# ConvNeXt-V2 block on one core: three of eleven blocks' hidden layer stored whole and read back, the rest rebuilt whole

## The chip, the cores and the metric

The kernel runs on one core of one Trainium2 chip. The metric is the device time of a whole execution in microseconds (us). The kernel before takes 1508.77 us, the median of 3 executions (1508.57 to 1510.78).

A **ratio** below is the mean time of one kernel's fast runs over the mean of the other's fast runs of the same rounds. It is therefore not quite the ratio of the medians that are quoted beside it. Its 95 % interval stands in brackets. "Same" means within 2 %.

## The reference

The input is 512 x 512 pixels of 96 channels in bf16; the hidden layer has 384 features.

```python
def reference(x, dw, w1, w2, grn_gamma, grn_beta):
    ...                                          # out = 3x3 depthwise convolution of x
    h = _layernorm(out, axis=-1)
    h = jnp.einsum('bhwc,ce->bhwe', h, w1)
    h = _gelu(h)
    gx = jnp.sqrt((h * h).sum(axis=(1, 2), keepdims=True) + 1e-6)
    nx = gx / (gx.mean(axis=-1, keepdims=True) + 1e-6)
    h = grn_gamma * (h * nx) + grn_beta + h
    h = jnp.einsum('bhwe,ec->bhwc', h, w2)
    return x + h
```

The sum in `gx` runs over the whole picture. No output can be made before the hidden layer of every pixel has been seen once, and neither kernel holds that layer (128 blocks of 1.57 MB) on the chip. So the kernel has two phases, and the question is what of the hidden layer phase 2 reads back and what it rebuilds.

## The kernel before

The picture is cut into 128 blocks of four rows, which are 2048 pixels. A block's hidden layer consists of four pixel quarters (`t`, `m`) of three feature chunks (`j`), each chunk a tile of 128 features by 512 pixels.

**Phase 1** works a slot at a time. In a slot, PE convolves one block (the input comes transposed from DVE) and makes the first product of a block a few slots older, ACT evaluates the gelu, and the sums of squares are taken. For quarters that have features on the partitions ("channel-major", `cm_quads`), DVE takes them with `bn_stats`. For the others PE takes them with a product of the tile with itself (`gram`). The normalized convolution yn goes to DRAM and comes back channel-major. In this kernel every block keeps one quarter of the hidden layer in DRAM:

```python
def cm_quads(q):
    return 2 if is_res(q) else 3          # is_res: the two last blocks
def kept_quads(q):
    return 2 if is_res(q) else 1
...
# one slot of phase 1, in this order
conv(0); unit(0, 2); unit(2, 1)
squares(0)                                # 2 statistics entries on DVE
conv(1, False)
turn_x(s + 2)                             # DVE transposes the input of a later slot
unit(3, 1); unit(4, 2)
squares(1)                                # 2 entries
...
squares(2)                                # 2 entries
...
squares_rest()                            # entries of the third quarter: 3
store = put_out                           # one quarter to g_dram in the next slot
```

**Phase 2** takes the blocks in turn. It loads the kept quarter (`gl`), yn of the three other quarters and the input (`xr`), rebuilds three quarters on PE and ACT (`gr`), makes the second product (`O`) and adds input and bias. The sum of input and bias (`xb`) is POOL's work:

```python
def stage_load(n, sq, pq):
    ...
        kept = late.gl.tile([128, 1, NCH, QW], bf16, name="gl")
        (pq if q % 3 == 0 else sq).dma_start(
            out=kept[:].rearrange("p t j w -> p (t j w)"), in_=g_dram[q])
        ynt = yn_ring[v]
        sq.dma_start(out=ynt[:, :, kept_quads(q) * 128:], in_=yn_rows(q))
    xr = late.xr.tile([128, PXP, C], bf16, name="xr")      # 5 buffers
    pq.dma_start(out=xr[:], in_=x[0, r0:r0 + GR]...)

def stage_xb(q, pq, bias):
    xb = late.xb.tile([128, PXP, C], f32, name="xb")
    pq.tensor_tensor(out=xb[:], in0=grp[q]["xr"][:], in1=bias[...], op=ALU.add)
...
for n, q in enumerate(ORDER):             # phase 2
    if n + PRE < NBLK:
        stage_load(n + PRE, nc.sync, nc.gpsimd)
    if n + 2 < NBLK:
        stage_xb(ORDER[n + 2], nc.gpsimd, B2c)
    ...
    o_sb = stage_mm2(n, q)                # second product; pace() puts rebuilding between
```

Of the kernel before, what the change touches and what calls it, by code (L numbers as in the profile page):

```python
# [12 lines left out]
GR = 4  # L13
# [5 lines left out]
RES = 2  # L19

# [33 lines left out]
def kernel(  # L54
# [29 lines left out]
    g_dram = dram.tile([NBLK, 128, NCH * QW], bf16, name="g_dram")  # L84
# [5 lines left out]

    def cm_quads(q):
        return 2 if is_res(q) else 3

    def kept_quads(q):
        return 2 if is_res(q) else 1
# [16 lines left out]
    def yn_rows(q):  # L112
        k = kept_quads(q) * 128
        return yn_dram[q:q + 2].rearrange("q c (r w) -> (q c) r w", r=GR)[0:128, :, k:]
# [29 lines left out]
    grp = {}  # L144
    res_g = {q: prepool.tile([128, 2, NCH, QW], bf16, name=f"resg{q}") for q in range(NBLK - RES, NBLK)}
# [7 lines left out]
    ORDER = list(range(NBLK - RES, NBLK)) + list(range(NBLK - RES))  # L153

    class late:
        pass
# [3 lines left out]
    with ExitStack() as p1:  # L160
        pe, dve, act, pool, sp = (InOrder(tc, e) for e in (nc.tensor, nc.vector, nc.scalar, nc.gpsimd, nc.sync))
        gshpool = p1.enter_context(tc.tile_pool(name="gsh", bufs=3))
        gmpool = p1.enter_context(tc.tile_pool(name="gm", bufs=3))
# [70 lines left out]
        def stage_load(n, sq, pq):  # L234
            q = ORDER[n]
            v = (ORDER[0] + n) % NYT
            r0 = q * GR
            if is_res(q):
                kept, ynt = res_g[q], ynts[q]
            else:  # L240
                kept = late.gl.tile([128, 1, NCH, QW], bf16, name="gl")
                (pq if q % 3 == 0 else sq).dma_start(
                    out=kept[:].rearrange("p t j w -> p (t j w)"), in_=g_dram[q])
                ynt = yn_ring[v]
                sq.dma_start(out=ynt[:, :, kept_quads(q) * 128:], in_=yn_rows(q))
# [3 lines left out]
            grp[q] = dict(kept=kept, ynt=ynt, xr=xr)  # L249

        def recompute_units(q):
            nk = kept_quads(q)
            ynt = grp[q]["ynt"]

            def fresh(j):
                if j == 0:
                    grp[q]["made"] = late.gr.tile([128, NCH, (NQ - 1) * QW], bf16, name="gr")
                def half(U, t0, t1):
                    for t in range(t0, t1):
                        pe.matmul(quad_out(U[:, t - t0, :]), lhsT=w1p[:, j * 128:(j + 1) * 128],  # L260
                                  rhs=quad(ynt[:], t), start=True, stop=True)
                    act.activation(out=grp[q]["made"][:, j, (t0 - nk) * QW:(t1 - nk) * QW],
                                   in_=U[:, :t1 - t0, :].rearrange("p k w -> p (k w)"), func=ACTF.Gelu_apprx_tanh)

                if not is_res(q):
                    half(late.psU2.tile([128, NQ - 1, QW], f32, name="U2"), nk, NQ)
                elif j % 2:
                    half(banks(1), nk, nk + 1)
                    half(banks(1), nk + 1, NQ)
                else:  # L270
                    half(banks(2), nk, NQ)

            return [lambda j=j: fresh(j) for j in range(NCH)]
# [9 lines left out]
        def stage_mm2(n, q):  # L283
            kept, made, xb = grp[q]["kept"], grp[q]["made"], grp[q]["xb"]
            nk = kept_quads(q)
            GQ = QW // 128
            o_sb = late.o.tile([128, PXP, C], bf16, name="o_sb")
            for sub in range(NSUB):
                O = late.psO.tile([128, GPS, C], f32, name="O")
                for gl_ in range(GPS):  # L290
                    gg = sub * GPS + gl_
                    for j in range(NCH):
                        t, c = gg // GQ, gg % GQ * 128
                        if t < nk:
                            lhsT = kept[:, t, j, c:c + 128]
                        else:
                            c += (t - nk) * QW
                            lhsT = made[:, j, c:c + 128]
# [4 lines left out]
                if n == NBLK - 1:  # L303
                    out_part(q, o_sb, sub)
# [18 lines left out]
        def advance(target, upto):  # L323
            while made[0] < total and made[0] < target and todo[made[0]] < upto:
                n = todo[made[0]]
                if not waiting:
                    waiting.extend(recompute_units(ORDER[n]))
# [530 lines left out]
        if store:  # L858
            store()
# [102 lines left out]
```

## Time and profile before

| kernel before | value |
|---|---|
| time, median | 1508.77 us |
| span of the profiled execution | 1504.8 us |
| mean granted clock of PE | 0.993 |
| busy: PE, DVE, ACT, POOL | 94 %, 79 %, 96 %, 87 % |
| last transpose of an input starts | 863.6 us |
| copy of `B2c` starts, after which phase 2's adds can start | 969.8 us |
| last add of an output tile starts | 1501.2 us |

The page's line of the chain that ended last gives each engine's share of the span:

```profile
POOL 22%; PE 20%; ACT 12%; DVE 10%; DMA 8%; issue 3%; SPq 3%; POOLq 0%; ACTq 0%
```

Every compute engine is on that chain; none can be neglected. The stretches, groups and instructions that carry the argument are shown in the prediction. One wait of phase 2 (1060 to 1460 us; total, times, longest) shows who is late there:

```profile
DVE o_sb L32 <- POOL xb L279: 87.4, 81, 3.5
```

### The profile page before, as it was taken

Reading aid. Unit: us, or ns where it says so; the run is one execution under the profiler, and the core shown is the slowest. Engines: PE = TensorE matmul, PEld = TensorE weight load, DVE = VectorE, ACT = ScalarE, POOL = GpSimd, SP = SyncE. Lnnn points to the kernel's source line nnn. Section 1 sums busy time; section 2 is a strip of 40 time slices with the busy share of each in tenths; the row PEclk is TensorE's granted clock in tenths of the full one; section 3 lists DMA queues with packets and bytes.
Section 4 is the critical chain, followed back from the end, with each engine's and each line's share of the span. In section 5 each row is a group of like instructions: output and inputs, shape, how many; then the busy total and the mean of one; then the engine's idle time right before and its main releaser. Section 6 shows DMA issues by size and latency. Waiting matters only on the chain.

```text
span 1504.8 us, 54858 instructions
## 1 busy us (share of the span) xinstructions
PE 1415.3 (94%) x23110; PEld 815.8 (54%) x23110; DVE 1193.5 (79%) x2149; ACT 1450.9 (96%) x1699; POOL 1309.6 (87%) x934
## 2 busy tenths in 40 slices
PE   8888999999999999999999987799999999999998
PEld 3434444444444444444444443477777777676776
DVE  7759999999999999999999999755555555455555
ACT  7898999999999999999999999899999999899997
POOL 3469899999999999989999987199999999899998
PEclk9999999999999999999999999999999999999999
DMA  6568787888888888888888777799999999999996
GB/s 177 175 199 255 227 257 241 252 260 242 245 256 250 256 260 244 252 252 249 248 265 243 221 216 252 237 340 388 378 391 385 380 378 376 362 367 382 378 378 237
DMA packets 235181, 427.10 MB, mean 284 GB/s; under 512 B 34006, under 2 KB 148278, under 8 KB 234934
## 3 DMA queue, kind: packets, MB, share of 16 engines
q1 hardware_dynamic: 219972, 356.59, 73.7%
q0 software_dynamic: 13600, 66.86, 11.7%
q8 instruction: 181, 2.97, 0.8%
q14 instruction: 66, 0.54, 0.1%
q10 hardware_dynamic: 1362, 0.15, 0.1%
HBM read 272.78 MB, written 150.72 MB: 281 GB/s over the span
## 4 chain that ended last, share of the span: by engine, by line
POOL 22%; PE 20%; ACT 12%; DVE 10%; DMA 8%; issue 3%; SPq 3%; POOLq 0%; ACTq 0%
POOL xb L279 13%; PE U L32 10%; PE O L32 9%; DVE bst L32 7%; ACT gsh L32 6%; ACT gm L32 4%; SPq L32 3%; POOL yn L32 3%; DMA ynT<-yn_dram 2%; DMA yn_dram<-yn 2%; ACT y_bf L32 2%; POOL ysq L32 2%; DMA xin<-in_x_dram 2%; DVE xT L32 2%; POOL xr L247 1%
## 5 line engine op out<-in xcount | busy, mean ns | idle before, releaser
L32 PE MATMUL U<-ynT,w1p 128*128 128x512 bf16 x2292 | 651.7, 381 | 37.3 <-ACT gsh L32 9.6
L32 ACT ACTIVATE gr<-U 128x1536 bf16<-128x1536 f32 (+1 forms) x386 | 519.3, 1449 | 13.5 <-PE U L32 12.8
L32 DVE BATCH_NORM_STATS2 bst<-gsh 128x6 f32<-128x512 bf16 x756 | 465.4, 673 | 20.0 <-ACT gsh L32 19.5
L32 DVE TENSOR_TENSOR o_sb<-O,xb 128x384 bf16<-128x384 f32 x512 | 277.7, 556 | 254.1 <-PE O L32 157.5
L32 POOL TENSOR_TENSOR yn<-y_bf,rbc 128x1536 bf16<-128x1536 bf16 x126 | 391.5, 3109 | 70.7 <-DMA rbc<-r_dram 26.4
L279 POOL TENSOR_TENSOR xb<-xr,B2c 128x1536 f32<-128x1536 bf16 x126 | 394.8, 3135 | 34.0 <-DVE B2c L32 27.2
L32 ACT ACTIVATE gm<-U 128x512 bf16<-128x512 f32 (+1 forms) x640 | 419.8, 803 | 3.9 <-PE U L32 3.8
L32 ACT ACTIVATE gsh<-U 128x1024 bf16<-128x1024 f32 x504 | 375.0, 872 | 5.7 <-PE U L32 4.1
L32 PE MATMUL Y<-xT,Wq 64*32 64x511 bf16 (+1 forms) x8694 | 321.7, 387 | 21.4 <-ACT y_bf L32 9.5
L32 POOL TENSOR_TENSOR ysq<-y_bf 128x1536 bf16<-128x1536 bf16 x114 | 314.1, 2756 | 11.4 <-ACT y_bf L32 11.4
L32 PEld LDWEIGHTS <-w1p 128*128 128x128 bf16 x2292 | 183.1, 98 | 241.3 <-issue 141.5
L32 PEld LDWEIGHTS <-gr 128*128 128x128 bf16 x4584 | 236.8, 98 | 106.3 <-issue 21.2
L32 PE MATMUL O<-W2s,gr 128*128 128x96 bf16 x4584 | 257.2, 206 | 11.5 <-DVE o_sb L32 11.0
L32 DVE BATCH_NORM_STATS2 bst<-gm 128x6 f32<-128x512 bf16 x378 | 232.9, 671 | 0.2 <-ACT gm L32 0.2
L32 PEld LDWEIGHTS <-Wq 64*32 64x32 bf16 x9216 | 113.1, 90 | 199.1 <-issue 150.5
L32 ACT ACTIVATE y_bf<-Y 128x1536 bf16<-128x1536 f32 x121 | 188.0, 1554 | 8.5 <-DMA gam_bf<-in_grn_gamma_dram 4.4
L32 DVE STREAM_TRANSPOSE xT<-xin 128x576 f32<-128x576 f32 (+1 forms) x256 | 181.2, 748 | 0.0
L32 PEld LDWEIGHTS <-gm 128*128 128x128 bf16 x1560 | 99.3, 98 | 84.9 <-issue 52.2
L32 PE MATMUL SG<-gm 128*128 128x128 bf16 x1560 | 130.3, 220 | 1.9 <-DVE SG L32 1.2
L32 PE MATMUL U<-w1p,ynT 128*128 128x384 bf16 (+2 forms) x780 | 127.3, 272 | 1.4 <-ACT resg L32 0.2
L247 POOL DMA_DIRECT2D xr<-in_x_dram x123 | 68.1, 554 | 38.5 <-POOL xb L279 35.6
L32 PE MATMUL O<-W2s,gl 128*128 128x96 bf16 x1512 | 85.4, 207 | 0.0
(105 smaller groups left out, 674.9 us busy)
## 6 DMA issues: line engine op xcount, KB each, us to landing
ynT<-yn_dram SPq DMA_DIRECT2D x254, 384.0 KB
xin<-in_x_dram SPq DMA_DIRECT2D x126, 432.0 KB
yn_dram<-yn SPq DMA_DIRECT2D x512, 96.0 KB
xr<-in_x_dram POOLq DMA_DIRECT2D x128, 384.0 KB, 6.6
out_dram<-o_sb SPq DMA_DIRECT2D x127, 384.0 KB
g_dram<-gsh SPq DMA_DIRECT2D x126, 384.0 KB
gl<-g_dram SPq DMA_DIRECT2D x84, 384.0 KB
gl<-g_dram POOLq DMA_DIRECT2D x42, 384.0 KB, 7.2
```

The source lines that it names most:

```text
L32: r = f(*a, **k)
L247: pq.dma_start(out=xr[:], in_=x[0, r0:r0 + GR].rearrange("r w c -> (r w) c").rearrange("(p g) c -> p g c", g=PXP))
L279: pq.tensor_tensor(out=xb[:], in0=grp[q]["xr"][:], in1=bias[:, None, :].to_broadcast([128, PXP, C]), op=ALU.add)
```

## The change

The intent is to cut transfers in small pieces and some rebuilding. Three blocks of every eleven (35 of 126) are stored whole, with four times the bytes a row, and are only read back. The 91 others are not stored. They read all of their yn and rebuild all four quarters, in units of one pixel quarter, with one activation of 1536 columns each. A whole block has all four quarters channel-major and the block after it only two, so that the mean stays at three. The diff, of which the cuts below are the core, also has the last two blocks rebuild all four quarters, stores a whole block in two halves, spreads the `gram` products differently, and holds three rebuilt and two read blocks in phase 2.

```diff
+WHOLE = (0, 4, 8)
+GRB = 3
...
+    def is_whole(q):
+        return not is_res(q) and q % 11 in WHOLE
     def cm_quads(q):
-        return 2 if is_res(q) else 3
+        return NQ if is_whole(q) else 2 if is_res(q) or (q - 1) % 11 in WHOLE else 3
...
         def stage_load(n, sq, pq):
+            if is_whole(q):
+                grp[q]["g"] = late.gl.tile([128, NQ, NCH, QW], bf16, name="gl")
+                pq.dma_start(out=grp[q]["g"][:].rearrange("p t j w -> p (t j w)"), in_=g_dram[whole.index(q)])
             else:
-                kept = late.gl.tile([128, 1, NCH, QW], bf16, name="gl")
-                (pq if q % 3 == 0 else sq).dma_start(
-                    out=kept[:].rearrange("p t j w -> p (t j w)"), in_=g_dram[q])
-                sq.dma_start(out=ynt[:, :, kept_quads(q) * 128:], in_=yn_rows(q))
+                if not is_res(q):
+                    sq.dma_start(out=ynt[:], in_=yn_rows(q))
...
+        def recompute(q, t):              # one quarter: three products, one activation
+            g, ynt = grp[q]["g"], grp[q]["ynt"]
+            ...
+                act.activation(out=g[:, t, j0:j0 + n, :], in_=U[:, :n, :], func=ACTF.Gelu_apprx_tanh)
...
             def squares_rest():
-                if px0(b):
+                for m in range(2, cm_quads(b)):
                     for j in range(NCH):
-                        entry(j, 2, gms[b][:, j * QW:(j + 1) * QW])
+                        entry(j, m)
...
+                if is_whole(b):
+                    stores.extend(((b, 0), (b, 1)))
```

More of the change, by code (lines that the diff above doesn't have):

```diff
@@ L83 @@
     dram = ctx.enter_context(tc.tile_pool(name="dram", bufs=1, space=bass.MemoryType.DRAM))
-    g_dram = dram.tile([NBLK, 128, NCH * QW], bf16, name="g_dram")
     yn_dram = dram.tile([NBLK, C, GR * W], bf16, name="yn_dram")
@@ L89, in is_res @@
         return q >= NBLK - RES
+    def is_whole(q):
+        return not is_res(q) and q % 11 in WHOLE
     def cm_quads(q):
-        return 2 if is_res(q) else 3
-    def kept_quads(q):
-        return 2 if is_res(q) else 1
+        return NQ if is_whole(q) else 2 if is_res(q) or (q - 1) % 11 in WHOLE else 3
+    whole = [q for q in range(NBLK) if is_whole(q)]
+    g_dram = dram.tile([len(whole), 128, NQ * NCH * QW], bf16, name="g_dram")
     def chans(i):
@@ L112, in yn_rows @@
     def yn_rows(q):
-        k = kept_quads(q) * 128
-        return yn_dram[q:q + 2].rearrange("q c (r w) -> (q c) r w", r=GR)[0:128, :, k:]
+        return yn_dram[q:q + 2].rearrange("q c (r w) -> (q c) r w", r=GR)[0:128]
     def yn_dst(q, r):
@@ L144 @@
     grp = {}
-    res_g = {q: prepool.tile([128, 2, NCH, QW], bf16, name=f"resg{q}") for q in range(NBLK - RES, NBLK)}
     NYT = 6
@@ L153 @@
     ORDER = list(range(NBLK - RES, NBLK)) + list(range(NBLK - RES))
+    nth_made = {}
+    for q in ORDER:
+        if not is_whole(q):
+            nth_made[q] = len(nth_made)
     class late:
-        pass
+        psU2 = None
     p2 = ExitStack()
@@ L161 @@
         pe, dve, act, pool, sp = (InOrder(tc, e) for e in (nc.tensor, nc.vector, nc.scalar, nc.gpsimd, nc.sync))
-        gshpool = p1.enter_context(tc.tile_pool(name="gsh", bufs=3))
-        gmpool = p1.enter_context(tc.tile_pool(name="gm", bufs=3))
+        gpool = p1.enter_context(tc.tile_pool(name="g", bufs=4))
         bstpool = p1.enter_context(tc.tile_pool(name="bst", bufs=2))
@@ L235, in stage_load @@
             q = ORDER[n]
-            v = (ORDER[0] + n) % NYT
             r0 = q * GR
-            if is_res(q):
-                kept, ynt = res_g[q], ynts[q]
-            else:
-                kept = late.gl.tile([128, 1, NCH, QW], bf16, name="gl")
-                (pq if q % 3 == 0 else sq).dma_start(
-                    out=kept[:].rearrange("p t j w -> p (t j w)"), in_=g_dram[q])
-                ynt = yn_ring[v]
-                sq.dma_start(out=ynt[:, :, kept_quads(q) * 128:], in_=yn_rows(q))
+            grp[q] = {}
+            if is_whole(q):
+                grp[q]["g"] = late.gl.tile([128, NQ, NCH, QW], bf16, name="gl")
+                pq.dma_start(out=grp[q]["g"][:].rearrange("p t j w -> p (t j w)"), in_=g_dram[whole.index(q)])
+            else:
+                ynt = yn_ring[(ORDER[0] + nth_made[q]) % NYT]
+                if not is_res(q):
+                    sq.dma_start(out=ynt[:], in_=yn_rows(q))
+                grp[q]["ynt"] = ynt
             xr = late.xr.tile([128, PXP, C], bf16, name="xr")
@@ L248, in stage_load @@
                 "(p g) c -> p g c", g=PXP))
-            grp[q] = dict(kept=kept, ynt=ynt, xr=xr)
-        def recompute_units(q):
-            nk = kept_quads(q)
-            ynt = grp[q]["ynt"]
-            def fresh(j):
-                if j == 0:
-                    grp[q]["made"] = late.gr.tile([128, NCH, (NQ - 1) * QW], bf16, name="gr")
-                def half(U, t0, t1):
-                    for t in range(t0, t1):
-                        pe.matmul(quad_out(U[:, t - t0, :]), lhsT=w1p[:, j * 128:(j + 1) * 128],
-                                  rhs=quad(ynt[:], t), start=True, stop=True)
-                    act.activation(out=grp[q]["made"][:, j, (t0 - nk) * QW:(t1 - nk) * QW],
-                                   in_=U[:, :t1 - t0, :].rearrange("p k w -> p (k w)"), func=ACTF.Gelu_apprx_tanh)
-                if not is_res(q):
-                    half(late.psU2.tile([128, NQ - 1, QW], f32, name="U2"), nk, NQ)
-                elif j % 2:
-                    half(banks(1), nk, nk + 1)
-                    half(banks(1), nk + 1, NQ)
-                else:
-                    half(banks(2), nk, NQ)
-            return [lambda j=j: fresh(j) for j in range(NCH)]
+            grp[q]["xr"] = xr
+        def recompute(q, t):
+            if t == 0:
+                grp[q]["g"] = late.gr.tile([128, NQ, NCH, QW], bf16, name="gr")
+            g, ynt = grp[q]["g"], grp[q]["ynt"]
+            for j0, n in ((0, NCH),) if late.psU2 else ((0, 2), (2, 1)):
+                U = late.psU2.tile([128, NCH, QW], f32, name="U2") if late.psU2 else banks(n)
+                for j in range(j0, j0 + n):
+                    pe.matmul(quad_out(U[:, j - j0, :]), lhsT=w1p[:, j * 128:(j + 1) * 128],
+                              rhs=quad(ynt[:], t), start=True, stop=True)
+                act.activation(out=g[:, t, j0:j0 + n, :], in_=U[:, :n, :], func=ACTF.Gelu_apprx_tanh)
         def stage_xb(q, pq, bias):
@@ L283, in stage_mm2 @@
         def stage_mm2(n, q):
-            kept, made, xb = grp[q]["kept"], grp[q]["made"], grp[q]["xb"]
-            nk = kept_quads(q)
+            g, xb = grp[q]["g"], grp[q]["xb"]
             GQ = QW // 128
@@ L293, in stage_mm2 @@
                         t, c = gg // GQ, gg % GQ * 128
-                        if t < nk:
-                            lhsT = kept[:, t, j, c:c + 128]
-                        else:
-                            c += (t - nk) * QW
-                            lhsT = made[:, j, c:c + 128]
-                        pe.matmul(O[:, gl_, :], lhsT=lhsT, rhs=W2s[:, j, :],
+                        pe.matmul(O[:, gl_, :], lhsT=g[:, t, j, c:c + 128], rhs=W2s[:, j, :],
                                    start=(j == 0), stop=(j == NCH - 1))
@@ L304, in stage_mm2 @@
                     out_part(q, o_sb, sub)
+                if sub == NSUB - 1 and not is_whole(q):
+                    used[0] += 1
                 pace(n, sub)
@@ L315 @@
         PRE = 5
-        UPB = NCH
-        LEAD = RES * UPB + 2
-        todo = [n for n in range(NBLK) for _ in range(UPB)]
+        LEAD = 5
+        todo = [(n, t) for n in range(NBLK) if not is_whole(ORDER[n]) for t in range(NQ)]
         total = len(todo)
-        made = [0]
-        waiting = []
+        made, used = [0], [0]
         def advance(target, upto):
-            while made[0] < total and made[0] < target and todo[made[0]] < upto:
-                n = todo[made[0]]
-                if not waiting:
-                    waiting.extend(recompute_units(ORDER[n]))
-                waiting.pop(0)()
+            while made[0] < total and made[0] < target:
+                n, t = todo[made[0]]
+                if n >= upto or nth_made[ORDER[n]] >= used[0] + GRB:
+                    break
+                recompute(ORDER[n], t)
                 made[0] += 1
         def pace(n, sub):
-            due = sum(1 for v in todo if v <= n + 1) if sub == NSUB - 1 else 0
+            soon = (n, sub + 2) if sub < NSUB - 1 else (n + 1, 1)
+            due = sum(1 for v in todo if v < soon or v[0] < n)
             even = LEAD + (n * NSUB + sub + 1) * total / (NSUB * NBLK)
@@ L619 @@
             e_ += cm_quads(q)
-        gms = {}
+        gs = {}
         TAIL = NCH * QW * (NQ - 2)
@@ L624, in px0, with tail @@
             return NCH * QW * (cm_quads(b) - 2)
+        def tail(b):
+            return gs[b][:, 2:].rearrange("p t j w -> p (t j w)")
         def mlp_units(b):
-            gsh = res_g[b] if is_res(b) else gshpool.tile([128, 2, NCH, QW], bf16, name="gsh")
-            gms[b] = gmpool.tile([128, TAIL], bf16, name="gm")
+            g = gs[b] = gpool.tile([128, NQ, NCH, QW], bf16, name="g")
             yt = ynts[b]
@@ L639, in unit @@
                         cm_mm(U[:, t - t0, :], j, t)
-                    act.activation(out=gsh[:, t0:t0 + n, j, :], in_=U[:], func=ACTF.Gelu_apprx_tanh)
+                    act.activation(out=g[:, t0:t0 + n, j, :], in_=U[:], func=ACTF.Gelu_apprx_tanh)
                     return
@@ L646, in unit @@
                     if c < px0(b):
-                        j, sz = c // QW, QW
-                        cm_mm(Uf[:, c - c0:c - c0 + sz], j, 2)
+                        t, j = divmod(c // QW, NCH)
+                        sz = QW
+                        cm_mm(Uf[:, c - c0:c - c0 + sz], j, 2 + t)
                     else:
@@ L656, in unit, with entry @@
                     c += sz
-                act.activation(out=gms[b][:, c0:end], in_=Uf, func=ACTF.Gelu_apprx_tanh)
-            def entry(j, m, src):
+                act.activation(out=tail(b)[:, c0:end], in_=Uf, func=ACTF.Gelu_apprx_tanh)
+            def entry(j, m):
                 k, e = divmod(ents[b] + m, 32)
@@ L662, in entry, with store_next, gram_next @@
                     bsts[k] = bstpool.tile([128, NCH, 32, 6], f32, name="bst")
-                dve.bn_stats(out=bsts[k][:, j, e, :], in_=src)
+                dve.bn_stats(out=bsts[k][:, j, e, :], in_=g[:, m, j, :])
             def squares(j):
                 for m in range(2):
-                    entry(j, m, gsh[:, m, j, :])
+                    entry(j, m)
             def squares_rest():
-                if px0(b):
+                for m in range(2, cm_quads(b)):
                     for j in range(NCH):
-                        entry(j, 2, gms[b][:, j * QW:(j + 1) * QW])
-            def store():
-                sp.dma_start(out=g_dram[b], in_=gsh[:, 0].rearrange("p j w -> p (j w)"))
-            return unit, squares, squares_rest, store
-        def gram_mms(b, part=None):
-            n = (TAIL - px0(b)) // E
-            for k in range(n) if part is None else range(n // 2) if part == 0 else range(n // 2, n):
-                for j in range(NCH):
-                    c = px0(b) + k * E + j * 128
-                    v = gms[b][:, c:c + 128]
-                    pe.matmul(gram[:, j, :], lhsT=v, rhs=v, start=False, stop=True, skip_group_check=True)
+                        entry(j, m)
+            return unit, squares, squares_rest
+        stores = []
+        def store_next():
+            if stores:
+                b, h = stores.pop(0)
+                n = NCH * QW * 2
+                sp.dma_start(out=g_dram[whole.index(b)][:, h * n:h * n + n],
+                             in_=gs[b][:, 2 * h:2 * h + 2].rearrange("p t j w -> p (t j w)"))
+        grams = []
+        def gram_next(n):
+            for b, k0 in grams[:n]:
+                for k in (k0, k0 + 1):
+                    for j in range(NCH):
+                        c = px0(b) + k * E + j * 128
+                        v = tail(b)[:, c:c + 128]
+                        pe.matmul(gram[:, j, :], lhsT=v, rhs=v, start=False, stop=True, skip_group_check=True)
+            del grams[:n]
         def combine(b):
@@ L728 @@
                 put(m, "combine", b)
-                put(m + (b < NBLK - 1), "gram", b)
                 last_slot = m
@@ L734 @@
         turn_x(1)
-        store = None
         for s in range(last_slot + 1):
@@ L747 @@
                 stage_rows(k)
-            if store:
-                store()
-                store = None
+            store_next()
             for k in get("newton"):
@@ L790 @@
                     stage_turn(k)
-                for b in get("gram"):
-                    gram_mms(b)
+                gram_next(2)
             else:
                 b = mlp[0]
-                unit, squares, squares_rest, put_out = mlp_units(b)
+                unit, squares, squares_rest = mlp_units(b)
                 conv = lambda n, fence=True: taps[n](fence) if taps else None
-                def gram_of_last(part):
-                    for b2 in get("gram"):
-                        if b2 != b:
-                            gram_mms(b2, part)
                 conv(0)
@@ L813 @@
                 squares(1)
-                gram_of_last(0)
+                gram_next(1 if taps else 2)
                 unit(6, 1)
@@ L822 @@
                     evac()
-                gram_of_last(1)
+                gram_next(1 if taps else 2)
                 unit(8, 2)
@@ L831 @@
                 squares_rest()
-                for b2 in get("gram"):
-                    if b2 == b:
-                        gram_mms(b2)
-                if not is_res(b):
-                    store = put_out
+                grams.extend((b, k) for k in range(0, (TAIL - px0(b)) // E, 2))
+                if is_whole(b):
+                    stores.extend(((b, 0), (b, 1)))
+                if b == NBLK - 1:
+                    gram_next(len(grams))
             if s == 0:
@@ L849 @@
                 late.xb = p2.enter_context(tc.tile_pool(name="xb", side="right", bufs=3))
-                late.gr = p2.enter_context(tc.tile_pool(name="gr", side="right", bufs=4))
-                late.gl = p2.enter_context(tc.tile_pool(name="gld", side="right", bufs=6))
+                late.gr = p2.enter_context(tc.tile_pool(name="gr", side="right", bufs=GRB))
+                late.gl = p2.enter_context(tc.tile_pool(name="gld", side="right", bufs=2))
                 late.o = p2.enter_context(tc.tile_pool(name="o", side="right", bufs=4))
@@ L857 @@
                     stage_xb(ORDER[n], pool, B2bc_f)
-        if store:
-            store()
+        while stores:
+            store_next()
         gsm = p2.enter_context(tc.tile_pool(name="gsm", side="right", bufs=1))
@@ L887 @@
                                        accum_out=rs_[:])
-        ahead = [f for n in range(RES) for f in recompute_units(ORDER[n])]
-        for f in ahead[:-1]:
-            f()
+        advance(3, RES)
         tot_ps = late.psO.tile([128, GPS, C], f32, name="O")[:, 0, 0:1]
@@ L905 @@
         dve.tensor_copy(out=B2c[:], in_=B2bc_f[:])
-        ahead[-1]()
-        made[0] = RES * UPB
+        advance(4, RES)
     with p2:
```

## The prediction

> **What bounds the kernel now.** I read the page first, then the busy time of each engine in stretches, then groups, waits and instructions in order of time. The span falls into phase 1 (convolution, norm, first product and statistics, to about 965 us) and phase 2 (rebuild the hidden layer, second product, output, from 970 us). One stretch of each:
>
> ```profile
> 360.00:460.00 100.00, 96.37 (x1741) 47.24 (x1733) 99.56 (x171) 100.00 (x144) 94.16 (x76) 1.00 0.85 250
> ...
> 1178.00:1278.00 100.00, 97.13 (x1368) 70.06 (x1366) 51.18 (x96) 98.06 (x73) 92.40 (x57) 1.00 1.03 377
> ```
>
> Columns: length, PE, PEld, DVE, ACT and POOL busy, granted clock, DMA share, GB/s. In phase 1 ACT never rests and DVE rests 0.4%: two engines are full. In phase 2 PE, ACT, POOL and the DMA engines are all above 92%. The groups between 1060 and 1460 us give the prices:
>
> ```profile
> L32 ACT ACTIVATE gr<-U 128x1536 bf16<-128x1536 f32 x288 | 391.9, 1462 | 9.4 <-PE U L32 8.9
> L279 POOL TENSOR_TENSOR xb<-xr,B2c 128x1536 f32<-128x1536 bf16 x96 | 300.9, 3135 | 1.9
> ...
> L247 POOL DMA_DIRECT2D xr<-in_x_dram x95 | 52.6, 554 | 30.8 <-POOL xb L279 27.9 <-issue 2.9
> L242 POOL DMA_DIRECT2D gl<-g_dram x31 | 16.6, 536 | 0.0
> ```
>
> POOL in order of time tells which of the four is full:
>
> ```profile
> 1107.66 0.56 POOL L247 DMA_DIRECT2D xr<-in_x_dram  x1 [0.30 <-POOL xb L279]
> 1108.21 0.54 POOL L242 DMA_DIRECT2D gl<-g_dram  x1
> 1108.76 3.13 POOL L279 TENSOR_TENSOR xb<-xr,B2c 128x1536 f32<-128x1536 bf16 x1
> 1112.19 0.55 POOL L247 DMA_DIRECT2D xr<-in_x_dram  x1 [0.30 <-POOL xb L279]
> 1112.77 3.14 POOL L279 TENSOR_TENSOR xb<-xr,B2c 128x1536 f32<-128x1536 bf16 x1
> 1116.20 0.56 POOL L247 DMA_DIRECT2D xr<-in_x_dram  x1 [0.30 <-POOL xb L279]
> 1116.78 3.14 POOL L279 TENSOR_TENSOR xb<-xr,B2c 128x1536 f32<-128x1536 bf16 x1
> 1120.22 0.55 POOL L247 DMA_DIRECT2D xr<-in_x_dram  x1 [0.30 <-POOL xb L279]
> ```
>
> POOL has no wait but the 0.30 us between an add and a following issue. A block costs 4.0 us, with a gl load 4.55; every third block has one, so 12.56 us for three, 4.18 a block. ACT needs 3 x 1.356 = 4.07 (8 activations took 10.85 us end to end), PE about 4.06. So **POOL** is the bound of phase 2, by only 3%.
>
> In phase 1 a slot lasts 7.03 us. DVE hands the next slot its transposed input:
>
> ```profile
> 375.61 1.42 DVE L32 STREAM_TRANSPOSE xT<-xin 128x576 f32<-128x576 f32 x2
> 378.64 0.88 PE L32 MATMUL Y<-xT,Wq 64*32 64x512 bf16 x24
> ...
> 381.07 2.77 DVE L32 BATCH_NORM_AGGREGATE mv<-bst 128x2 f32<-128x192 f32 x3
> 384.89 1.42 DVE L32 STREAM_TRANSPOSE xT<-xin 128x576 f32<-128x576 f32 x2
> 385.67 0.89 PE L32 MATMUL Y<-xT,Wq 64*32 64x512 bf16 x24 [0.15 <-ACT y_bf L32]
> ```
>
> The slot's first convolution matmul that needs the new input is the seventh. Counting 0.70 us for the first transpose and 0.25 for six matmuls, the slack is 3.03 - 0.45 = 2.6 us before the aggregate and 0.78 - 0.45 = 0.3 after it. The aggregates (every 10 or 11 slots) use up the slack, DVE earns some 0.25 us a slot back, and no PE wait for a transpose is listed. DVE fits just barely.
>
> **What the Trainium skill says.** "ScalarE: Activation LUTs", What ACT_TABLE_LOAD costs: 186 ns + 0.833 ns an element, 93 ns overlap; for 1536 that is 1466, the trace has 1462, and 1.356 end to end against 1.373. "DMA: Bandwidth & Descriptors", Anatomy of one DMA: descriptor generation is a small part and many descriptors can be issued before it shows; the trace has only one size on this queue (536 ns for 128 rows), so whether rows four times as long cost the same is untested. Same page, Why small descriptors are slow: a fixed overhead for each packet. The trace agrees in kind: between 1060 and 1460 us the second-smallest packets (768 B of yn) are 49,000 of 83,000, and subtracting the big ones at the POOL queue's speed leaves about 36 ns for each, 21.6 GB/s an engine against 24.1 (an estimate). "SBUF — State Buffer", Who interferes with whom: a DVE instruction with one SBUF input does not hold up GpSimd; xb takes 3127 to 3143 ns all through phase 2 while DVE adds from PSUM, which agrees.
>
> **The change, part by part.** Before, every block kept one quarter in DRAM and rebuilt three. Now 35 of 126 blocks keep all four, 91 none, and the two last blocks rebuild all four, not two.
>
> Phase 2, ACT and PE: rebuilt quarters were 126 x 3 + 2 x 2 = 382 and are 93 x 4 = 372. ACT: 32 activations in 11 blocks x 1.356 = 43.4, 3.95 a block. PE: 32 groups of three matmuls at 0.65 and 44 groups of twelve at 0.51 (starts in order of time) are 43.2, with the small seams of the trace about 3.99 a block.
>
> Phase 2, POOL: the built order per 11 blocks has 11 adds, 11 xr issues, 3 gl issues (all gl now on this queue), and only 8 changes from an add to an issue, since adds and issues partly come in pairs. 11 x 3.11 + 11 x 0.56 + 3 x 0.54 + 8 x 0.30 = 34.2 + 6.2 + 1.6 + 2.4 = 44.4, so 4.04 a block, if the large gl issue still costs 0.54.
>
> Phase 2, DMA: a block moved 4 x 393 KB = 1.573 MB; now yn 524 KB x 91/126 = 379, gl 1573 x 35/126 = 437, xr and out 393 each: 1.602 MB. Packet time falls about 2%, as 768 B rows become 4096 B ones. At 4.1 us that is 391 GB/s, and short stretches of the trace show 400. A gl load is issued four to five blocks, some 16 us, ahead of use, where 393 KB land in 7.3 us.
>
> With three engines within 2.5% I don't expect the largest alone: 4.10 a block where 4.18 was, x 123 blocks = **-10 us**.
>
> Between phases: 15 banks instead of 18 are rebuilt before the first second product, 3 x 0.45 us: **-1 us**.
>
> Phase 1: ACT work is the same. Statistics entries are 383 for 382. But they bunch: DVE takes 12 between the transposes of a whole block and the next block's, 6 after that, else 9 as before. At 0.591 us each and 1.34 for the transposes a slot's DVE work is 8.43, 4.89 or 6.66 against 7.03. So each whole block takes 1.4 us from the slack, and an aggregate 2.62 more. I ran the ledger over the built order of both kernels (slack = old slack + 7.03 - work, at most 2.6; below zero it is a stall that ACT feels). Before: 1 us of stall in 104 slots, which fits a trace with none. After: about eleven stalls of 0.5 to 1.8 us, mostly where whole block and aggregate meet, 14 us in all; PE's lead over ACT swallows some 0.25 of each. **+11 us.** The stores are bunched too (786 KB in two slots of three or four), but are read only in phase 2; DMA share is 0.85 and I charge nothing.
>
> Sum: 1508.8 - 10 - 1 + 11 = 1509; as the ledger errs on the high side, I say **1508 us**.
>
> **Rivals.** (1) The DVE burst is hidden, so only phase 2 counts: 1497, or 1485 if ACT's 3.95 is reached. For it: slack is mostly above 1.4. Against: the saw-tooth that touches zero. (2) The gl issue grows with its bytes: 4 x 0.54 makes POOL 44.4 + 4.8 = 49.2 per 11 blocks, 4.47, 36 us more than before: 1555. For it: nothing measured. Against: the row count stays 128. (3) DMA becomes the bound of phase 2: 1.602 MB at today's 377 GB/s are 4.25 a block, +9 where I have -10: 1528. For it: a share of 1.03 already. Against: no compute engine waits for a load in phase 2, and packets get larger. (4) Large loads come late and PE stalls at whole blocks, 1 us each: +35, 1543. Against: 16 us of lead.
>
> **Range and chances.** Gains and losses cancel and each is bounded near 15 us, so I put 1490 to 1528 at eight in ten. Faster by 2% (under 1478.6) needs ACT's pace and a free phase 1, and still more: 4%. Slower by 2% (over 1538.9) needs rival 2 or 4: 7%. Within 2%: 89%.
>
> **What would show it.** Right: PE waits for DVE transposes in phase 1 (some 10 us, about one for every third whole block), ACT there about 1.3% less busy; xb starts 4.04 to 4.10 apart on average, gl issues near 0.54 us, the DMA share no higher. Wrong: ACT still full in phase 1; a gl issue of 1 us or more; PE idle on gl; or phase 2 shorter by more than 20 us.

## More of the kernel before

"Half clock" names the stretches in which the trace shows a granted clock of PE of 0.5.

In phase 2, `nc.gpsimd` leaves it to the scheduler where POOL's instructions stand against each other; the names `pe`, `act`, `pool` of phase 1 keep the order of the program.

## The result

The changed kernel takes **1512.43 us** (1510.07 to 1513.74, 4 runs) against 1508.67 (1508.45 to 1510.78, 4 runs) of the kernel before. The ratio is 1.002 [1.0003, 1.0037]: the same. The result is correct. The mean granted clock of its four runs is 0.987 to 0.991, where the profiled run of before had 0.993.

The total says little, because a gain and a loss of some 25 us each cancel. The events, from the instructions in order of time, lie as follows:

| event | before, us | after, us | later by |
|---|---|---|---|
| last transpose of an input starts | 863.6 | 884.6 | 21.0 |
| copy of `B2c` starts | 969.8 | 996.9 | 27.1 |
| last add of an output tile starts | 1501.2 | 1503.9 | 2.7 |
| end of the span | 1504.8 | 1508.2 | 3.4 |

Phase 1 with the passage between the last convolutions and phase 2 lost 27.1 us. From `B2c` to the last add it took 531.4 us before and 507.0 us after, a gain of 24.4 us.

**Phase 2.** Two stretches of the changed kernel, one in each phase, with the columns as in the prediction (length, PE, PEld, DVE, ACT and POOL busy, clock, DMA share, GB/s):

```profile
360.00:460.00 100.00, 95.69 (x1729) 46.88 (x1722) 98.32 (x169) 99.01 (x142) 91.43 (x65) 1.00 0.83 250
1160.00:1260.00 100.00, 99.97 (x1431) 73.67 (x1430) 55.12 (x101) 99.77 (x74) 96.22 (x57) 1.00 1.02 405
```

In phase 2 PE was 97.13 % busy and is now 99.97 %; ACT has risen with it. In phase 1 ACT, which never rested, now rests 1 %. The chain that ended last of the changed kernel:

```profile
PE 32%; DMA 1%; DVE 0%; issue 0%; DVEq 0%
```

It can be followed back only through phase 2, a third of the span, and in that third it is PE alone. POOL, 22 % before, is not on it, and DVE's wait for `xb` has fallen from 87.4 us to

```profile
DVE o_sb L34 <- POOL xb L271: 2.6, 4, 0.7
```

The groups between 1060 and 1460 us of the changed kernel (busy us, mean ns of one, idle time before and what ended it):

```profile
L34 ACT ACTIVATE gr<-U 128x1536 bf16<-128x1536 f32 x295 | 401.0, 1458 | 1.3 <-PE U L34 0.3 <-ACT gr L34 0.2
L271 POOL TENSOR_TENSOR xb<-xr,B2c 128x1536 f32<-128x1536 bf16 x101 | 315.4, 3134 | 1.7 <-DVE o_sb L34 0.2
L252 POOL DMA_DIRECT2D xr<-in_x_dram x101 | 55.8, 553 | 15.9 <-POOL xb L271 13.1 <-issue 2.9
L245 POOL DMA_DIRECT2D gl<-g_dram x27 | 14.4, 533 | 0.0
```

The prices are those of before: an activation 1458 ns, an add 3134, an issue 553. The `gl` issue moves four times the bytes for 533 ns, where it was 536. What has fallen is the idle time of POOL before its `xr` issues: 13.1 us for 101 blocks, where it was 27.9 for 95. POOL of the changed kernel in order of time:

```profile
1157.84 0.55 POOL L252 DMA_DIRECT2D xr<-in_x_dram  x1 [0.30 <-POOL xb L271]
1158.39 0.53 POOL L245 DMA_DIRECT2D gl<-g_dram  x1
1158.94 6.21 POOL L271 TENSOR_TENSOR xb<-xr,B2c 128x1536 f32<-128x1536 bf16 x2
1165.09 1.10 POOL L252 DMA_DIRECT2D xr<-in_x_dram  x2
```

Adds and issues now partly come in pairs, and the second line of a pair, and the pair of issues at 1165.09, follow without a gap. The mean distance of two `xb` starts (over the 100 distances from the 11th to the 111th add, here and below) fell from 4.207 to **3.987 us**.

The DMA engines moved 403 GB/s between 1060 and 1460 us, where it was 377, at about the same share. In that stretch the packets under 2 KB fell from 54,878 to 4,801.

**Phase 1.** One place, after a whole block, with DVE, PE and ACT in order of time:

```profile
400.02 7.18 DVE L34 BATCH_NORM_STATS2 bst<-g 128x6 f32<-128x512 bf16 x12
406.70 0.41 PE L34 MATMUL Y<-xT,Wq 64*32 64x512 bf16 x6
407.11 1.43 DVE L34 STREAM_TRANSPOSE xT<-xin 128x576 f32<-128x576 f32 x2
407.92 0.85 PE L34 MATMUL Y<-xT,Wq 64*32 64x512 bf16 x18 [0.81 <-DVE xT L34]
409.54 3.90 ACT L34 ACTIVATE g<-U 128x1024 bf16<-128x1024 f32 x6 [0.99 <-ACT g L34]
```

Twelve statistics entries stand in a row, 7.18 us, a whole slot's time. The transposes begin only at 407.11. PE runs the six convolution matmuls that need no new input, waits 0.81 us, and ACT feels 0.99 us of it. The list of waits between 200 and 900 us (total, times, longest) has nine such:

```profile
PE Y L34 <- DVE xT L34: 11.4, 9, 1.8
```

Before there was none. The nine gaps of ACT that answer to them add to 13.7 us.

**The passage.** The changed kernel between the last convolutions and phase 2, cut from the answers for SP, POOL, PE and ACT (SPq is SP's issuing):

```profile
951.29 0.53 POOL L34 DMA_DIRECT2D gl<-g_dram  x1
951.88 2.61 SPq L34 DMA_DIRECT2D yn_dram<-yn  x4
...
962.07 0.54 POOL L245 DMA_DIRECT2D gl<-g_dram  x1
971.89 0.32 SPq L34 DMA_DIRECT2D ynT<-yn_dram  x1
976.62 1.89 PE L34 MATMUL U<-ynT,w1p 128*128 128x512 bf16 x4 [6.79 <-DMA ynT<-yn_dram]
977.74 12.20 ACT L34 ACTIVATE g<-U 128x1024 bf16<-128x1024 f32 x18 [6.31 <-issue]
```

A small write of yn issued at 951.88 had landed only when SP could issue the read that waits for it, at 971.89. PE then waited 6.79 us for the read and ACT 6.31. SP's waits for such writes in the stretch around the passage, first of before (915 to 960 us), then of the changed kernel (940 to 985 us):

```profile
SPq L32 <- DMA yn_dram<-yn: 15.1, 10, 6.7
```

```profile
SPq L34 <- DMA yn_dram<-yn: 22.5, 10, 16.2
```

The longest grew from 6.7 to 16.2 us. Two whole-block loads of 1.57 MB each, issued from POOL at 951.29 and 962.07, ran in the same time, and landed at 964.36 and 973.19; the trace's DMA records put the packets of the small write between 959 and 971. From the last transpose to `B2c` it took 106.2 us before and 112.4 after, 6 us more.

### The profile page after: what moved, and what is told of

Read it like the earlier page. It is cut to its first block, busy times and chain, and to the rows that moved or that the text cites. A ratio compares the mean times of both kernels' runs of the same rounds, so it can differ in the third digit from the quotient of the medians.

```text
span 1508.2 us, 54153 instructions
## 1 busy us (share of the span) xinstructions
PE 1410.5 (94%) x23065; PEld 813.2 (54%) x23065; DVE 1201.2 (80%) x2152; ACT 1440.1 (95%) x1689; POOL 1302.6 (86%) x927
## 5 line engine op out<-in xcount | busy, mean ns | idle before, releaser
L34 ACT ACTIVATE g<-U 128x512 bf16<-128x512 f32 (+1 forms) x1152 | 759.5, 835 | 34.4 <-PE U L34 18.4
L34 DVE BATCH_NORM_STATS2 bst<-g 128x6 f32<-128x512 bf16 x1149 | 697.4, 674 | 45.6 <-ACT g L34 44.8
L34 PE MATMUL U<-ynT,w1p 128*128 128x512 bf16 x2265 | 639.2, 382 | 42.0 <-ACT g L34 14.6
L34 ACT ACTIVATE gr<-U 128x1536 bf16<-128x1536 f32 (+1 forms) x376 | 506.2, 1444 | 4.4 <-PE U L34 2.1
L34 POOL TENSOR_TENSOR yn<-y_bf,rbc 128x1536 bf16<-128x1536 bf16 x126 | 391.1, 3105 | 87.7 <-DMA rbc<-r_dram 43.4
L34 PEld LDWEIGHTS <-gr 128*128 128x128 bf16 x4464 | 220.1, 98 | 65.0 <-issue 0.7
L34 PE MATMUL O<-W2s,gr 128*128 128x96 bf16 x4464 | 235.7, 206 | 0.3 <-DVE o_sb L34 0.3
L34 PEld LDWEIGHTS <-g 128*128 128x128 bf16 x1548 | 98.1, 98 | 82.4 <-issue 53.2
L34 PE MATMUL SG<-g 128*128 128x128 bf16 x1548 | 127.9, 221 | 2.6 <-DVE SG L34 2.2
L34 PEld LDWEIGHTS <-gl 128*128 128x128 bf16 x1680 | 82.8, 98 | 23.4 <-issue 0.8
L34 PEld LDWEIGHTS <-ynT 128*128 128x128 bf16 x774 | 61.0, 98 | 28.4 <-issue 9.3
## 6 DMA issues: line engine op xcount, KB each, us to landing
gl<-g_dram POOLq DMA_DIRECT2D x35, 1536.0 KB, 10.7
```

The source lines that it names most:

```text
L34: r = f(*a, **k)
```

## The experiments

**Theory** after reading the result: phase 2 gained because POOL was relieved and fewer quarters are rebuilt; phase 1 lost because DVE's statistics are bunched; the passage lost because the early `gl` loads delay a yn write. **Rivals:** phase 1 lost to the bunched stores, or to the granted clock (about 36 us of half clock in the changed kernel's trace, about 24 before); phase 2 gained by the larger packets alone.

Ten kernels ran, in three sets. Each set ran on one chip and shares its runs of the kernel before: median 1507.46 us (1505.06 to 1509.82) for the first four, 1507.52 (1504.12 to 1515.20) for the next four, 1515.32 (1504.14 to 1521.67) for the last two. All were correct. By the 2 % rule all but one (two blocks of eleven, slower) are "same" as the kernel before; a difference counts below where the interval of its ratio leaves out 1, which experiment 8 and the first kernel of experiment 5 do not. Four totals came out 0.2 to 3 us below their expected range (experiments 1 to 4), two above: four blocks of eleven by 3.6 us and experiment 7 by 1.9.

### 1. The statistics spread over two slots

The changed kernel, with the fourth quarter's three entries of a whole block put off to the slot of the block after it:

```diff
             def squares_rest():
+                for f in late_sq:
+                    f()
+                late_sq.clear()
                 for m in range(2, cm_quads(b)):
                     for j in range(NCH):
-                        entry(j, m)
+                        if m == 3:
+                            late_sq.append(lambda j=j: entry(j, 3))
+                        else:
+                            entry(j, m)
...
-                combine(b)
+                if not is_whole(b):
+                    combine(b)
```

> The changed kernel, but the three statistics entries of a whole block's fourth quarter wait until the next block's slot, so DVE takes 9 entries between all transposes, never 12 and 6. DVE-burst theory: the nine ACT stalls of 1.0 to 2.6 us between 250 and 870 us (13.7 us together) vanish, no PE wait for a DVE transpose is left, phase 1 gets 11 to 14 us shorter, total 1499 to 1501. Rival (bunched stores delay the rows that norm and the first product read; DVE only fills the hole): stalls stay, total 1510 to 1513. Rival (the lower granted clock): stalls stay where the clock halves.

It took 1498.83 us (1494.59 to 1502.35), ratio 0.9943 [0.9919, 0.9968]. The waits of PE between 200 and 900 us that are left there:

```profile
PE SG L34 <- POOL ysq L34: 6.3, 6, 2.1
PE Y L34 <- ACT y_bf L34: 2.9, 15, 0.7
PE U L34 <- ACT g L34: 2.7, 4, 1.1
```

No wait for a DVE transpose is left (the one for POOL's `ysq` is new), and `B2c` comes at 986.5 us, 10.4 earlier. The stores are untouched and half clock is still about 36 us, so neither rival made these stalls. SP's longest wait at the passage stayed (17.1 us).

### 2. The first whole-block loads behind the last yn read

The changed kernel, with the loads that run ahead of phase 2 put on SP's queue, where they stand behind the yn reads:

```diff
-                pq.dma_start(out=grp[q]["g"][:]..., in_=g_dram[whole.index(q)])
+                (sq if n <= 6 else pq).dma_start(out=grp[q]["g"][:]..., in_=g_dram[whole.index(q)])
```

> The changed kernel, but the first two whole-block loads (1.57 MB each) go to the SP queue, behind the last read of yn, instead of running ahead on POOL's queue. Theory (these loads delay the landing of the last yn write, for which SP waited 16.2 us and ACT 6.3): SP's wait falls to the 7 us of the kernel before, the ACT stall near the end of phase 1 to 1 us or less, total 5 to 8 us shorter, 1504 to 1507. Rival (the yn chain is late because POOL's norm is late): the stall stays, total 1510 to 1513.

It took 1501.78 us (1500.24 to 1503.17), ratio 0.9964 [0.9948, 0.9979]. SP's waits from 940 to 985 us, and ACT in order of time:

```profile
SPq L34 <- DMA yn_dram<-yn: 11.8, 6, 8.2
```

```profile
954.52 27.06 ACT L34 ACTIVATE g<-U 128x1024 bf16<-128x1024 f32 x42
```

The longest wait is halved, and ACT runs 42 activations without the 6.31 us gap. `B2c` comes at 988.6 us, 8.3 earlier. The nine waits for transposes are there again, 11.4 us. So the passage and the stalls are separate losses.

### 3. Both repairs

> Both edits together. If the two theories hold and the gains add, phase 1 and the passage to phase 2 cost no more than in the kernel before and phase 2 keeps its 24 us: total 1491 to 1496, below both kernels. If the gains share a cause, 1499 to 1505.

It took **1489.83 us** (1489.32 to 1490.24), ratio 0.9885 [0.9870, 0.9899], which beats both kernels. `B2c` comes at 974.9 us and `xb` starts lie 3.985 us apart. Against the changed kernel's ratio of 1.002 the two repairs took off 0.0077 and 0.0056 alone, together 0.0133, and 0.0135 in one kernel: within the intervals, some 0.0025 to either side, they add.

### 4. The kernel before, all `gl` loads issued by SP

```diff
-                (pq if q % 3 == 0 else sq).dma_start(
+                sq.dma_start(
```

> The kernel before with all its g loads on the SP queue, so POOL has only adds and xr issues, 4.0 us a block. If POOL's 4.18 alone bound phase 2, it falls to the next bound, ACT 4.07 and PE 4.06: xb starts 4.08 to 4.10 apart (4.21 before), total 1493 to 1498. Rival (DMA bound at 377 GB/s with 768 B rows, POOL busy beside it): starts stay near 4.2, total 1506 to 1511.

It took 1490.1 us (1488.91 to 1496.76), ratio 0.9901 [0.9874, 0.9929]. One stretch of its phase 2:

```profile
1160.00:1260.00 100.00, 100.00 (x1421) 73.68 (x1419) 55.19 (x99) 100.00 (x76) 91.09 (x51) 1.00 1.04 391
```

PE and ACT fill up, POOL falls to 91 %, and `xb` starts lie 4.060 us apart. From `B2c` to the last add it takes 516.4 us, 15.0 less than before. So relief of POOL alone, without any of the change, is worth 15 of the 24.4 us. The remaining 9 are the step from 516.4 to 507.0 us, in which PE and ACT, full in both, have fewer groups to rebuild; that this is why is argued from the counts (0.07 us a block by the prediction's sums for PE, 9 us over 123 blocks), and larger packets were not tested apart from it. Larger packets are not needed for the first part, as here they were as small as before.

### 5. One more `xr` buffer, in both kernels

The wait of 0.30 us was thought to be a wait for the add just ended, whose end frees the `xr` buffer. The edit was the same in the kernel before and in that of experiment 3:

```diff
-                late.xr = p2.enter_context(tc.tile_pool(name="xr", side="right", bufs=5))
+                late.xr = p2.enter_context(tc.tile_pool(name="xr", side="right", bufs=6))
```

> The kernel before with a sixth xr buffer and nothing else. Theory: the 0.30 us before each xr issue is a wait for the add just ended to free the buffer; with one more buffer it waits for an older add, so POOL needs 3.69 us a block plus 0.54 for every third, 3.87, and is no longer the bound: xb starts 4.06 apart as with all g loads on SP, total 1488 to 1493. Rival (the 0.30 is a fixed cost of going from an add to an issue): starts stay at 4.18 to 4.21, total 1506 to 1511.

> The changed kernel with both mends and a sixth xr buffer: POOL falls to about 3.85 us a block. Theory (PE alone bounds phase 2 of the changed kernel now): xb starts stay at 3.985 us, total 1488 to 1491. Rival (POOL shares the bound): starts 3.93 to 3.96, total 1483 to 1487.

The first took 1505.52 us (1504.61 to 1507.25), ratio 0.9977 [0.9948, 1.0006], with 4.210 us between `xb` starts and all its 0.30 us gaps. The second took 1490.51 us (1488.21 to 1496.61), ratio 0.9882 [0.9846, 0.9918], as experiment 3 did. This looks like a refutation and is none. In the built order the scheduler had used the extra buffer to move every `xr` issue up by one add, so that it stood again right behind the add that frees its buffer (94 such waits between 1060 and 1460 us, as in the kernel before). The second had PE full already. The pair is **inconclusive**.

### 6. Four and two blocks of eleven

The kernel of experiment 3 with `WHOLE = (0, 3, 6, 9)` and with `WHOLE = (0, 5)`. In the second the repair of the passage covers the first load only: block 5 is the eighth of phase 2, so `n <= 6` leaves its load on POOL.

```diff
-WHOLE = (0, 4, 8)
+WHOLE = (0, 3, 6, 9)      # second kernel: (0, 5)
```

> The changed kernel with both mends and blocks 0, 3, 6 and 9 of eleven whole. PE falls to 3.75 us a block and ACT to 3.45 (28 groups instead of 32); the bytes grow to 1.69 MB a block. DMA theory (405 GB/s is near the limit): starts 4.1 to 4.2, PE waits for gl, total 1502 to 1515. POOL theory (DMA still has room): starts 3.95 to 4.02 as POOL has 4 gl issues in eleven, total 1486 to 1494.

> The changed kernel with both mends and blocks 0 and 5 of eleven whole: 36 groups to rebuild in eleven blocks, ACT 36 x 1.356 = 48.8 us or 4.44 a block, PE 4.2. ACT becomes the bound: starts 4.40 to 4.47, PE idle on ACT, phase 2 some 57 us longer, total 1540 to 1552. If PE and ACT were not what the number of whole blocks sets, starts stay near 4.0.

They took 1518.64 us (1514.98 to 1521.41), ratio 1.0061 [1.0029, 1.0093], and 1548.36 us (1546.16 to 1552.55), ratio 1.0264 [1.0224, 1.0303]. One stretch of each, four of eleven first:

```profile
1160.00:1260.00 100.00, 92.16 (x1373) 68.83 (x1370) 52.73 (x98) 88.43 (x64) 93.53 (x60) 1.00 1.02 413
```

```profile
1160.00:1260.00 100.00, 99.37 (x1310) 69.91 (x1308) 49.94 (x92) 100.00 (x75) 85.38 (x52) 1.00 0.95 341
```

With four, PE falls to 92 % and ACT to 88 % while the DMA engines move 413 GB/s. A block then moves 524 KB of yn x 7/11 + 1573 KB x 4/11 + 2 x 393 KB = 1.692 MB, which at 413 GB/s is 4.10 us, and 4.135 were measured. As the rate is that of the same kernel, this only agrees. That the transfers are the bound is read from the rest of the engines and from a wait between 1060 and 1460 us that the kernel of experiment 3 does not list:

```profile
DVE o_sb L34 <- DMA out_dram<-o_sb: 70.7, 38, 5.4
```

DVE waits for output tiles to be written before it can reuse their buffers, and PE waits for DVE (34.7 us), not for `gl`, as had been expected. With two, ACT is full: 36 activations of 1.356 us for eleven blocks are 4.44 us a block, and 4.410 were measured. Its total holds a second loss: the one load left on POOL, issued at 950.28, went with a wait of PE for a yn read of 7.7 us and an ACT gap of 7.3 us at the passage, which were 6.79 and 6.31 in the changed kernel. So the loss of the passage came back with half of its repair. Three of eleven is the best of these. Its 1.602 MB a block would take 3.88 us at 413 GB/s (an estimate), only some 3 % less than the 3.985 that PE needs.

### 7. The kernel before, POOL of phase 2 in program order

To move the issue away from the add that frees its buffer without any other change, POOL's instructions of phase 2 were given in order:

```diff
-                stage_load(n + PRE, nc.sync, nc.gpsimd)
+                stage_load(n + PRE, nc.sync, pool)
...
-                stage_xb(ORDER[n + 2], nc.gpsimd, B2c)
+                stage_xb(ORDER[n + 2], pool, B2c)
```

The built streams of all other engines are those of the kernel before. Each `xr` issue stands one add later, so the add that frees its buffer has ended an add ago.

> The kernel before with POOL's phase 2 in program order, the other four engines' streams unchanged. The sixth buffer of e6 settled nothing, as the built order moved each xr issue up behind the very add that frees its buffer again; here each issue follows the add after that one. Wait theory: the 0.30 us are gone, POOL needs 3.87 us a block, xb starts fall to the next bound, 4.06, total 1488 to 1493. Fixed-cost theory: the 0.30 stay, starts 4.18 to 4.21, total 1505 to 1511.

It took 1494.87 us (1492.09 to 1500.98), ratio 0.9870 [0.9811, 0.9929]; the kernel before scattered widely on this chip. POOL in order of time:

```profile
1153.71 3.13 POOL L32 TENSOR_TENSOR xb<-xr,B2c 128x1536 f32<-128x1536 bf16 x1
1156.78 0.56 POOL L32 DMA_DIRECT2D xr<-in_x_dram  x1
1157.59 3.12 POOL L32 TENSOR_TENSOR xb<-xr,B2c 128x1536 f32<-128x1536 bf16 x1 [0.25 <-DVE o_sb L32]
```

The 0.30 us gap before the issue is gone. The gap that is left waits for an output add of DVE, so POOL has become the follower. `xb` starts lie 4.036 us apart, and PE and ACT are 99.98 % busy. The wait theory that the extra buffer could not test is confirmed.

### 8. The changed kernel again

> The changed kernel once more, as a control with a second trace. The stalls of a DVE burst and of the late yn write should be at the same instructions (nine ACT stalls between 250 and 870 us, one of some 6 us just before phase 2), since they follow from the program; halvings of the clock should fall elsewhere in part. Total 1509 to 1514, xb starts 3.985 apart.

It took 1513.84 us (1513.23 to 1515.64), ratio 1.0003 [0.9954, 1.0052]. The nine waits for transposes are there at the same instructions, 11.4 us in all, and ACT's gap at the passage is 7.23 us. The half clock (about 42 us) fell partly elsewhere. The losses belong to the kernel and not to one execution.

## Why the prediction was right, point by point

The predicted time, 1508.0 us, is 4.4 us from the result and the class is right. Three terms carried it, and all three were wrong in size; that the number came so close is luck, as two large errors cancelled. Gain and loss were said to be bounded near 15 us each and were 24.4 and 27.1. Of the prediction's own signs of being wrong, one came: phase 2 is shorter by more than 20 us, with `xb` starts below the 4.04 to 4.10 that it named.

- **POOL bounds phase 2 before.** Right. Experiments 4 and 7 relieve POOL in two different ways, and each gains 14 to 15 us from `B2c` to the last add. The pace of before was put at 4.18 us a block and is 4.207 over the phase. A single stop of POOL, 2.88 us before the issue at 1306.98, is 0.03 us on each of the 100 distances, which is the difference. It is listed only as "issue", and I can't explain it. The kept traces show where it comes: before POOL's 114th DMA issue, whatever its tile and its time (1304 to 1405 us), for 2.47 to 2.89 us in ten of the twelve traces. In the other two (experiment 7 and four of eleven) an add of POOL ran up to that issue, so that a stop would be hidden. (The 3127 to 3143 ns of `xb` "all through phase 2" are those of 1060 to 1460 us; over the whole phase they are 3112 to 3147.)
- **Phase 2, "4.10 a block where 4.18 was, x 123 blocks = -10 us".** The sign was right, the size was not: -24.4 us. The failed step is "With three engines within 2.5% I don't expect the largest alone: 4.10". The largest alone is what came: 3.987 us measured, against PE's worked-out 3.99. Engines that are nearly equally full did not add to each other here; whether the buffers between them, which hold several blocks, are the reason was not tested. POOL's 4.04 was also mis-sized: 8 gaps for eleven blocks were counted, but the trace has 13.1 / 0.30 = 44 in 101 blocks, 4.8 for eleven, which makes 43.4 us or 3.95 a block. With the right gaps POOL would not have stood in PE's way.
- **The `gl` issue (rival 2).** Refuted: 533 ns for four times the bytes.
- **Transfers (rivals 3 and 4).** Refuted for this kernel: 403 GB/s at no higher share, and no PE idle on `gl` in phase 2. The rival's mistake was to take 377 GB/s for a limit. Experiment 6 reaches 413 to 415 with the transfers as the bound, close by.
- **The burst is hidden (rival 1).** Refuted by the nine waits. Its "1485 if ACT's 3.95 is reached" is a slip: 1485 belongs to PE's 3.99, and 3.95 would give about 1480.
- **Between phases, "-1 us".** Wrong in sign: +6 us from the last transpose to `B2c`. The step counted the rebuilding saved and left out that the first whole-block loads now run ahead on POOL's queue into the passage, where a yn write is waited for. Rival 4 looked for large loads that come late; these did harm by coming early. Experiment 2 recovers 8.3 us. Whether the saved rebuilding is worth 1 us can't be told: the stretch is 104.1 us there, and 103.9 to 108.2 in the four traces of the kernel before and its variants.
- **Phase 1, "+11 us".** The mechanism was right to the instruction: six matmuls run, the seventh waits. About eleven stalls of 14 us were predicted, and there were nine waits of PE with 13.7 us of ACT gaps. The term was still too small, as the last transpose starts 21 us later. Experiment 1 takes away 10.4 us by spreading three entries. About 5 us of the rest came early in phase 1, partly beside half clock at 191 us and with POOL waiting 17.0 us for `rbc`, where it waited 6.1 before. That these caused it is only argued, and the other traces speak against the half clock alone: at the transpose that is 5.0 us late at 255 us, experiment 3 is 1.9 us late, but experiment 8, at full clock from 125 to 548 us, 7.0. The charge of nothing for the bunched stores stood for the stalls.

What stays **open**: those 5 us; the lower mean clock of the changed kernel (0.987 to 0.991), which follows from more half clock, though whether idle gaps of PE caused it was not tested (13.7 of the 36 us lie at the passage, where experiment 2 has none, but experiment 3, without the long wait too, has 13.7); and the stop before the 114th issue.

## What to carry to other kernels

Moving work about at equal totals is not free on an engine without slack: twelve instructions in a row cost what nine and nine did not, and an entry put off by a slot gave it back. A prefetch on another queue shares the DMA engines with whatever small write and read the critical chain waits for, so here it belonged behind them. Before a large rearrangement, look for the full engine's own small waits: one line that moved issues off POOL, or two that put them one add later, brought the old kernel to 1490.1 and 1494.87 us (on two chips), where the whole change with both repairs reached 1489.83.

## What the Trainium skill lacked or had wrong

- "DMA: Bandwidth & Descriptors", Anatomy of one DMA: it has descriptor generation as a small part, and the trace agrees (536 ns for 384 KB, 533 ns for 1536 KB, 128 rows each). Its fit, 2.0 us + bytes / 436 GB/s, gives 2.9 and 5.6 us for these loads (an estimate from that page), where 7.2 and 10.7 us from issue to landing were measured with the engines full. It has no figure for a DMA among full queues; here a small write took up to 20 us to be seen as landed (951.88 to 971.89).
- Same page, Issuing engines are not separate DMA queues: transfers interleave whichever engine starts them, and experiment 2 agrees. It calls the time saved on the sequencer usually small beside the transfer. Here the issuing engine was the bound, and moving 0.54 us issues from it to SP gained 17.4 us between the medians (1507.46 to 1490.1).
- "GPSIMD Engine Reference", Instruction dispatch: an instruction's completion gates what waits on its semaphore and not the next instruction on POOL. The trace agrees: an issue that waits for the add just before it starts 0.30 us after that add, and one that doesn't follows without a gap. The page has no figure for this.
- "TensorE: Matmul & The Clock Gate", What's actually happening: half clock is named after an idle window of about 3.4 us. Here it also came with shorter PE gaps: 2.44 us (kernel before, ended at 1311.33; clock 0.57 in the mean from 1312 to 1316) and 1.67 us (changed kernel, ended at 191.13; clock 0.53 already from 190.90, and 0.51 from 191 to 194.4). Three first-product matmuls of the kernel before took 1.23 us there in place of 0.81.
- No page has a stop of POOL at a certain DMA issue: 2.47 to 2.89 us before the 114th in ten of the twelve traces.
